# Whole TensorE tiles in place of partial ones, in a kernel of windowed attention and gated attention experts

## The chip, the cores and the metric

The kernel runs on one core of a Trainium2 chip. Its engines work side by side: TensorE (PE) multiplies matrices and writes to PSUM, VectorE (DVE), ScalarE (ACT) and GpSimd (POOL) work element by element, and SyncE (SP) issues most DMA transfers. The time is the device time of one execution in microseconds (us).

A matmul is two instructions of TensorE: the weight load (PEld) puts one operand into the array, the matmul streams the other through it. The page writes their sizes as rows*columns of the array used (32*64, 128*128), then the shape of the streamed operand (partitions x elements).

## The reference

Two stages follow each other. First a sliding window attention of 8 batches and 8 heads over 576 positions with head dimension 64; then four attention experts over the 512 joined features, of which a gate picks two for each position.

```python
# stage 1: q, k, v are (8, 8, 576, 64) in fp32
scores = (q @ k.transpose(0, 1, 3, 2)) / sqrt(64)
mask = abs(pos[:, None] - pos[None, :]) <= 32
attn = softmax(where(mask, scores, -1e9))
x = (attn @ v).transpose(0, 2, 1, 3).reshape(8, 576, 512)

# stage 2: 4 experts, head dimension 64
logits = x @ w_gate
topk, w = the two largest logits of each position, softmax of the two
for e in range(4):
    q, k, v = x @ wq[e], x @ wk[e], x @ wv[e]
    a = softmax(where(causal, -1e9, q @ k.transpose(0, 2, 1) / sqrt(64)))
    ye = a @ v @ wo[e]
    out += (e in topk) * w * ye
```

A sequence of 576 positions is four and a half tiles of 128. The half tile at the end is what most of this case is about.

## The kernel before

The work is cut into named steps, and the list `ORDER` says in which order they are issued. Each engine runs its own instructions in that order. `S.i.h` is half `h` of the window scores of head group `i` (four heads; two groups to a batch), `U` and `E` the products with v, `T` the turning of the attention's result, `QK`, `V`, `PS`, `AV`, `PT`, `Y` the expert's projections, scores, products, transposes and output, `G1` and `G3` the gate, `w18` eighteen warm-up matmuls. The digits after the colon name which of four PSUM slots (two banks each) a step gets. `load`, `turn`, `loadv` and `dup` bring q, k and v in; a load of q or k may be issued once VectorE has turned the one three head groups before.

Window scores. Keys are on the output partitions, queries stream. The four heads of a group lie on four groups of 32 partitions, and the head dimension is cut in two halves `dh`. Each entry of `BLK` is (first key, keys, first query, last query); an entry of 128 keys fills the output's 128 partitions, one of 64 keys half of them.

```python
BLK = [[[(0, 128, 0, 128)], [(128, 64, 64, 192), (192, 64, 128, 256)], [(256, 64, 192, 256)]],
       [[(256, 128, 256, 384)], [(512, 128, 448, 576)], [(384, 64, 320, 448), (448, 64, 384, 512)]]]
CUT = [0, 256, 576]

def win_scores(b, g, half):
    ...
    for blocks in BLK[half]:
        for dh in range(2):
            for k0, n, lo, hi in blocks:
                p0 = k0 % 128
                for hh in range(4):
                    r = slice(32 * hh, 32 * hh + 32)
                    nc.tensor.matmul(sl[hh // 2][p0:p0 + n, hh % 2, lo - c0:hi - c0],
                                     KT[r, dh, k0:k0 + n], QT[r, dh, lo:hi],
                                     start=(dh == 0), stop=(dh == 1), skip_group_check=True)
    for p in range(2):
        ap = A[:, 2 * p:2 * p + 2, c0:c1]
        nc.scalar.activation(ap, sl[p][:, :, 0:c1 - c0], EXP, scale=scale_att)
        # then the mask, on GpSimd (on VectorE for the first two head groups)
```

The attention's result `XN` is [128 positions, tile, 512 features]. The fifth tile has only 64 positions, so the two head groups share it: group 0 in partitions 0 to 63, group 1 in 64 to 127. Turning it, 128 features at a time:

```python
def win_turn(b, dt):                      # four times for a batch
    pt = slot("tx")...
    for t in range(4):
        nc.tensor.transpose(pt[:, 128 * t:128 * t + 128], XN[:, t, 128 * dt:128 * dt + 128], ident)
    r = slice(64 * (dt // 2), 64 * (dt // 2) + 64)
    nc.tensor.transpose(pt[:, 512:576], XN[r, 4, 128 * (dt % 2):128 * (dt % 2) + 128], ident[r, r])
    nc.scalar.copy(XTF[:, dt, 0:S], pt[:, 0:S])
    nc.gpsimd.tensor_copy(X[b][:, dt, :], XTF[:, dt, 0:S])      # bf16
```

The experts, two at a time (`j`), where the size of a tile is `nrow(t) = min(128, 576 - 128 * t)`:

```python
def moe_proj_qk(b, j, n):   # for each 288 positions: 4 matmuls, 128 weights columns, whole tiles
    ...
def moe_proj_v(b, part):    # part 0: tiles 0 to 3; part 1: tile 4, n = 64
    ...
            nc.tensor.matmul(o, XTB[:, dt, 128 * t:128 * t + n], WV[:, dt, :], ...)

def moe_scores(b, j, c):
    ...
            nc.tensor.matmul(ps[0:rows, eo, at:at + hi - lo],
                             QKE[r, 1, 128 * kt:128 * kt + nrow(kt)], QKE[r, 0, lo:hi], ...)

def moe_av(b, j):
    for eo in range(2):
        for qt in range(NQT):                       # NQT = 5
            n = nrow(qt)
            for kt in range(qt + 1):
                nk = nrow(kt)
                o = off(kt, 128 * qt)
                nc.tensor.matmul(po[0:n, eo, 65 * qt:65 * qt + 65], ATE[0:nk, eo, o:o + n],
                                 VE[0:nk, kt, 2 * j + eo, :], start=(kt == 0), stop=(kt == qt))
    # then normalised and weighted by VectorE, into OE

def moe_turn(b, j):
    for qt in range(NQT):
        n = nrow(qt)
        nc.tensor.transpose(pt[:, 128 * qt:128 * qt + n], OE[0:n, qt, :, :]..., ident_bf[:n, :n])
    nc.vector.tensor_copy(OTT[:, j, :], pt[:, 0:S])

def moe_y(b, t0):           # two tiles at a time, the fifth alone
    for t in tiles:
        n = nrow(t)
        for j in range(2):
            nc.tensor.matmul(py[0:n, t - t0, :], OTT[:, j, 128 * t:128 * t + n], WO[:, j, :], ...)
    # ScalarE copies py to ysb, SyncE sends it out
```

Of the kernel before, what the change touches and what calls it, by code (L numbers as in the profile page):

```python
# [22 lines left out]
    load.0.qn.0 load.0.kn.0 loadv.0.0 load.1.kn.0 turn.0.qn.0 load.1.qn.0 turn.0.kn.0 dup.0.0.3 dup.0.0.1  # L23
    dup.0.0.0 dup.0.0.2 load.0.qn.1 w18:2 S.0.0:01 turn.1.kn.0 load.0.kn.1 loadv.0.1 dup.0.1.1 turn.1.qn.0
    w17:2 U.0.0:1 w8:3 S.1.0:02 turn.0.qn.1 WL.q load.2.qn.0 turn.0.kn.1 dup.0.1.2 dup.0.1.0 load.2.kn.0
    w9:1 S.1.1:20 load.3.qn.0 dup.0.1.3 S.0.1:13 U.1.0:0 U.1.1:1 E.0:3 WC.q U.0.1:0 T.0.3:3 w1:1 T.0.1:0
    T.0.0:3 T.0.2:1 turn.2.qn.0 turn.2.kn.0 w8:0 QK.0.0.0:1 load.3.kn.0 WL.v S.2.0:30 turn.3.qn.0
    turn.3.kn.0 loadv.1.0 load.4.qn.0 QK.0.0.1:1 QK.0.1.0:3 S.3.0:02 PS.0.0.0:3 QK.0.1.1:1 load.4.kn.0 WC.v
    S.2.1:02 G1.0:1 PS.0.1.0:3 PS.0.0.1:0 V.0.0:2 dup.1.0.3 dup.1.0.1 G3.0 dup.1.0.0 dup.1.0.2 S.3.1:03
    V.0.1:2 turn.4.qn.0 U.2.0:1 PS.0.1.1:0 turn.4.kn.0 PS.0.0.2:3 U.2.1:2 U.3.0:0 load.5.kn.0 PS.0.1.2:3  # L30
    late.0 U.3.1:1 PS.0.0.3:2 load.5.qn.0 E.1:3 S.4.0:20 T.1.2:3 turn.5.kn.0 T.1.3:1 turn.5.qn.0 T.1.0:2
    loadv.2.0 T.1.1:0 AV.0.0:3 PS.0.1.3:0 S.4.1:21 G1.1:0 S.5.0:23 G3.1 load.6.qn.0 QK.1.0.0:1 load.8.qn.0
    dup.2.0.2 load.6.kn.0 turn.6.qn.0 V.1.0:2 load.7.kn.0 dup.2.0.0 dup.2.0.3 QK.1.0.1:0 turn.6.kn.0
    dup.2.0.1 load.8.kn.0 S.5.1:13 QK.1.1.0:2 PS.1.0.0:1 U.4.1:0 QK.1.1.1:2 PS.1.0.1:1 S.6.0:03 U.5.1:2
    PS.1.1.0:0 PT.0.0:1 E.2:3 V.1.1:2 load.7.qn.0 PS.1.0.2:0 turn.7.qn.0 U.5.0:1 S.6.1:23 U.4.0:0 loadv.3.0
    WL.o PS.1.0.3:2 load.9.kn.0 T.2.2:1 turn.7.kn.0 T.2.3:3 PS.1.1.1:2 load.10.qn.0 T.2.0:0 T.2.1:1
    turn.8.qn.0 AV.0.1:3 dup.3.0.0 S.7.0:10 dup.3.0.3 G1.2:2 PS.1.1.2:3 turn.8.kn.0 G3.2 QK.2.0.0:1
    dup.3.0.2 dup.3.0.1 V.2.0:0 S.7.1:13 QK.2.0.1:2 PS.1.1.3:1 AV.1.0:0 S.8.0:21 loadv.4.0 U.7.1:3
    load.9.qn.0 turn.9.kn.0 PS.2.0.0:0 V.2.1:2 QK.2.1.0:1 dup.4.0.0 PS.2.0.1:0 load.11.qn.0 U.6.1:3 E.3:1
    QK.2.1.1:2 PS.2.0.2:1 load.10.kn.0 WC.o U.7.0:0 U.6.0:2 PS.2.1.0:1 PT.1.0:0 T.3.3:3 load.11.kn.0 T.3.1:2  # L40
    turn.9.qn.0 T.3.0:1 dup.4.0.2 loadv.5.0 PT.0.1:3 S.8.1:20 PS.2.0.3:3 AV.1.1:1 T.3.2:0 turn.10.qn.0
    dup.4.0.3 load.12.qn.0 dup.4.0.1 turn.10.kn.0 S.9.0:32 Y.0.0:0 PT.1.1:3 PS.2.1.1:1 AV.2.0:2 PS.2.1.2:1
    QK.3.0.0:0 G1.3:3 S.9.1:01 QK.3.0.1:2 G3.3 Y.0.2:0 V.3.0:1 PS.2.1.3:0 load.12.kn.0 PS.3.0.0:3 U.9.0:2
    E.4:0 PS.3.0.1:3 QK.3.1.0:1 S.10.0:02 turn.11.kn.0 Y.0.4:1 turn.11.qn.0 QK.3.1.1:3 PS.3.0.2:2 U.9.1:0
    PS.3.1.0:3 V.3.1:1 Y.1.0:2 U.8.1:1 PS.3.0.3:3 U.8.0:0 PS.3.1.1:3 dup.5.0.2 S.10.1:12 PT.2.0:0 AV.2.1:3
    T.4.1:1 T.4.2:2 turn.12.kn.0 dup.5.0.3 loadv.6.0 T.4.0:0 turn.12.qn.0 T.4.3:1 PS.3.1.2:2 dup.6.0.1
    load.13.kn.0 Y.1.2:3 G1.4:1 S.11.0:20 V.4.0:3 G3.4 PT.2.1:0 AV.3.0:2 PS.3.1.3:3 QK.4.0.0:1 dup.5.0.1
    dup.5.0.0 S.12.0:30 QK.4.0.1:2 load.13.qn.0 Y.1.4:3 V.4.1:1 QK.4.1.0:0 PS.4.0.0:1 S.11.1:32 dup.6.0.0
    load.15.qn.0 QK.4.1.1:0 PS.4.0.1:3 PT.3.0:1 U.10.1:2 PS.4.1.0:1 U.11.0:0 PS.4.0.2:2 U.11.1:3 dup.6.0.2
    S.12.1:01 load.15.kn.0 E.5:3 U.10.0:2 PS.4.0.3:1 T.5.2:3 turn.13.kn.0 load.14.kn.0 PS.4.1.1:0 T.5.3:1  # L50
    loadv.7.0 T.5.0:2 turn.13.qn.0 Y.2.0:3 T.5.1:0 PS.4.1.2:1 AV.3.1:2 S.13.0:03 AV.4.0:1 load.14.qn.0
    PT.3.1:3 PS.4.1.3:2 QK.5.0.0:0 G1.5:2 dup.6.0.3 turn.14.kn.0 S.13.1:30 QK.5.1.0:1 QK.5.0.1:3 G3.5
    AV.4.1:1 turn.15.kn.0 PS.5.0.0:3 QK.5.1.1:2 Y.2.2:0 PS.5.0.1:1 V.5.0:3 PS.5.1.0:1 E.6:2 U.12.1:0
    PS.5.1.1:1 PS.5.0.2:2 U.13.0:3 dup.7.0.1 Y.2.4:0 turn.15.qn.0 Y.3.0:1 U.13.1:3 PS.5.1.2:0 V.5.1:2
    dup.7.0.0 U.12.0:1 PS.5.0.3:0 T.6.3:2 PT.4.0:3 T.6.2:0 T.6.0:2 turn.14.qn.0 T.6.1:3 S.15.0:01 PS.5.1.3:3
    Y.3.2:2 dup.7.0.3 G1.6:0 QK.6.0.0:3 G3.6 S.14.0:21 QK.6.1.0:3 dup.7.0.2 PT.4.1:0 S.15.1:12 QK.6.0.1:0
    U.15.0:1 S.14.1:23 PS.6.0.0:1 AV.5.0:0 V.6.0:3 PS.6.0.1:1 Y.3.4:0 QK.6.1.1:2 V.6.1:1 E.7:0 U.14.1:3
    PS.6.1.0:0 PS.6.0.2:1 U.14.0:2 U.15.1:3 PS.6.1.1:1 T.7.0:2 PT.5.0:0 T.7.3:3 T.7.1:1 PS.6.0.3:2 T.7.2:0
    AV.5.1:3 PS.6.1.2:0 Y.4.0:2 QK.7.0.0:1 PT.5.1:3 AV.6.0:2 PS.6.1.3:3 QK.7.0.1:1 Y.4.2:3 QK.7.1.0:0
    PS.7.0.0:1 Y.5.0:3 QK.7.1.1:0 PS.7.0.1:1 G1.7:2 PS.7.1.0:0 PS.7.0.2:1 AV.6.1:3 G3.7 Y.4.4:0 V.7.0:1  # L60
    PS.7.0.3:3 PS.7.1.1:0 PT.6.0:2 Y.5.2:3 V.7.1:0 PS.7.1.2:2 PT.6.1:1 AV.7.0:0 PS.7.1.3:2 Y.5.4:1 AV.7.1:0
    Y.6.0:1 PT.7.0:2 PT.7.1:2 Y.7.0:2 Y.6.2:1 Y.7.2:1 Y.6.4:2 Y.7.4:2
# [6 lines left out]
S = 576  # L69
# [6 lines left out]
def kernel(  # L76
# [30 lines left out]
    xp = ctx.enter_context(tc.tile_pool(name="xp", bufs=1))  # L107
    mp = ctx.enter_context(tc.tile_pool(name="mp", bufs=2))
    atep = ctx.enter_context(tc.tile_pool(name="atep", bufs=3))
# [91 lines left out]
    def late_constants():  # L201
        nc.scalar.copy(ident_bf, ident)

    XTF = consts.tile([128, NDT, 640], F32, name="XTF")
    nc.gpsimd.memset(XTF[:, :, S:640], 0.0)

# [37 lines left out]
    def cast_weights(n):  # L244
# [4 lines left out]
        else:  # L249
# [5 lines left out]

    BLK = [[[(0, 128, 0, 128)], [(128, 64, 64, 192), (192, 64, 128, 256)], [(256, 64, 192, 256)]],
           [[(256, 128, 256, 384)], [(512, 128, 448, 576)], [(384, 64, 320, 448), (448, 64, 384, 512)]]]
    CUT = [0, 256, 576]

    AT, X, st = {}, {}, {}  # L260
# [15 lines left out]
    def win_scores(b, g, half):  # L276
# [6 lines left out]
        for blocks in BLK[half]:  # L283
            for dh in range(2):
                for k0, n, lo, hi in blocks:
                    p0 = k0 % 128
                    for hh in range(4):
                        r = slice(32 * hh, 32 * hh + 32)
                        nc.tensor.matmul(sl[hh // 2][p0:p0 + n, hh % 2, lo - c0:hi - c0],  # L289
                                         KT[r, dh, k0:k0 + n], QT[r, dh, lo:hi],  # L290
                                         start=(dh == 0), stop=(dh == 1), skip_group_check=True)
# [42 lines left out]
    def win_turn(b, dt):  # L334
        pt = slot("tx")[:, :, :].rearrange("p a c -> p (a c)")
        for t in range(4):
            nc.tensor.transpose(pt[:, 128 * t:128 * t + 128], XN[:, t, 128 * dt:128 * dt + 128], ident)  # L337
        r = slice(64 * (dt // 2), 64 * (dt // 2) + 64)
        nc.tensor.transpose(pt[:, 512:576], XN[r, 4, 128 * (dt % 2):128 * (dt % 2) + 128], ident[r, r])  # L339
        nc.scalar.copy(XTF[:, dt, 0:S], pt[:, 0:S])  # L340
        if b not in X:
            X[b] = xp.tile([128, NDT, S], BF16, name="XTB", tag="XTB")
        nc.gpsimd.tensor_copy(X[b][:, dt, :], XTF[:, dt, 0:S])  # L343
# [53 lines left out]
    def moe_proj_qk(b, j, n):  # L397
        XTB = X[b]
        if n == 0:
            st["QK", b, j] = mp.tile([128, 2, S], BF16, name="QKE", tag="QKE")  # L400
        QKE = st["QK", b, j]
# [6 lines left out]
        o = QKE[:, n, :].rearrange("p (a c) -> p a c", c=HS)  # L408
# [5 lines left out]
    def moe_proj_v(b, part):  # L414
        XTB = X[b]
        if part == 0:
            VE = mp.tile([128, NQT, 4, 65], BF16, name="VE", tag="VE")
            nc.gpsimd.memset(VE[:, :, :, 64:65], 1.0)
            st["VE", b] = VE
        VE = st["VE", b]  # L420
        base, tiles = ((0, (0, 1, 2, 3)), (4, (4,)))[part]
        pv_ = slot("pv")
        for t in tiles:
            n = nrow(t)
            o = pv_[0:n, (t - base) // 2, 256 * (t % 2):256 * (t % 2) + 256]
            for dt in range(NDT):
                nc.tensor.matmul(o, XTB[:, dt, 128 * t:128 * t + n], WV[:, dt, :],  # L427
                                 start=(dt == 0), stop=(dt == NDT - 1))
        if part == 0:
            nc.vector.tensor_copy(VE[:, 0:4, :, 0:64],  # L430
                                  pv_[:, :, :].rearrange("p a (t e d) -> p (a t) e d", e=4, d=64))
        else:
            nc.vector.tensor_copy(VE[0:64, 4, :, 0:64],
                                  pv_[0:64, 0, 0:256].rearrange("p (e d) -> p e d", d=64))

    def moe_scores(b, j, c):
        QKE = st["QK", b, j]
        if c == 0:
            st["ATE", b, j] = atep.tile([128, 2, 1600], BF16, name="ATE", tag="ATE")
# [220 lines left out]
```

## Time and profile before

| What | Value |
|---|---|
| Time, median of three runs | 282.28 us (280.27 to 282.44) |
| Span of the profiled execution | 281.2 us |
| PE busy | 266.3 us, 95% |
| Weight loads | 192.1 us, 68% |
| DVE, ACT, POOL busy | 170.5, 162.5, 145.4 us |
| Moved by DMA | 40.59 MB, mean 144 GB/s |

The chain of work that ended last, followed back from the last instruction, is 82% TensorE. A busy time counts an instruction from its start to its end, and matmuls overlap, so that busy times of TensorE say less than the distances between starts. The page's second part cuts the span in 40 slices of 7 us and gives each engine a digit, the tenths of the slice in which it is busy; PEclk is the clock that TensorE was granted, in tenths of full speed.

### The profile page before, as it was taken

The numbers are of one execution on the slowest core, as the hardware profiler recorded it, in microseconds if no ns is written. First come the engines' busy times: TensorE is split into PE (matmuls) and PEld (weight loads), VectorE is DVE, ScalarE is ACT, GpSimd is POOL, SyncE is SP. The second block draws the span as 40 slices with busy tenths as digits, with TensorE's granted clock in tenths as the row PEclk, the third lists the DMA queues.
The fourth block names the chain that finished last, engine by engine and source line by source line (L and its number), as shares of the span: only waits on it lengthen the run. The fifth ranks groups of instructions, "written<-read, shape, count | busy, mean of one in ns | idle before, by whom it ended". The sixth has DMA issues, their size and how long they took to land.

```text
span 281.2 us, 11384 instructions
## 1 busy us (share of the span) xinstructions
PE 266.3 (95%) x4909; PEld 192.1 (68%) x4925; DVE 170.5 (61%) x538; ACT 162.5 (58%) x241; POOL 145.4 (52%) x190
## 2 busy tenths in 40 slices
PE   8979899999999999999999999999999999999762
PEld 2547677777777877777776877787677777666420
DVE  6468854875867767495847725758872364446410
ACT  0527449754657647774667278834776547486142
POOL 6110338977848783497329836774076744302100
PEclk9999999999999999999999999999999999999668
DMA  6989999999998995940549639860222000231236
GB/s 147 228 202 219 205 179 215 216 193 226 228 194 214 202 227 105 205 127 33 135 127 215 166 92 183 164 171 2 77 97 77 2 21 2 78 149 46 69 123 213
DMA packets 76562, 40.59 MB, mean 144 GB/s; under 512 B 47072, under 2 KB 71648, under 8 KB 76512
## 3 DMA queue, kind: packets, MB, share of 16 engines
q1 hardware_dynamic: 75616, 39.28, 62.3%
q8 instruction: 38, 0.62, 1.0%
q10 hardware_dynamic: 896, 0.59, 0.9%
q14 instruction: 12, 0.10, 0.1%
HBM read 30.42 MB, written 9.44 MB: 142 GB/s over the span
## 4 chain that ended last, share of the span: by engine, by line
PE 82%; DMA 8%; DVE 4%; SPq 2%; ACT 2%; issue 1%; ACTq 0%
PE sc L289 17%; PE pp L405 11%; PE po L473 9%; PE u L316 9%; PE py L506 7%; PE tx L337 7%; PE pv L427 6%; PE ps L447 5%; DMA qn<-in_q_dram 5%; PE pg L361 3%; PE pt L495 3%; PE tx L339 2%; SPq L136 2%; DMA kn<-in_k_dram 2%; PE u L327 1%
## 5 line engine op out<-in xcount | busy, mean ns | idle before, releaser
L296 POOL TENSOR_TENSOR AT<-AT,MASKP 128x512 f32<-128x512 f32 (+1 forms) x56 | 77.6, 1407 | 41.6 <-ACT AT L294 41.5
L450 ACT ACTIVATE ATE<-ps 128x1024 bf16<-128x1024 f32 (+1 forms) x64 | 52.9, 837 | 30.9 <-PE ps L447 30.6
L294 ACT ACTIVATE AT<-sc 128x512 f32<-128x512 f32 (+1 forms) x64 | 38.1, 647 | 37.5 <-PE sc L289 37.4
L289 PE MATMUL sc<-Tqn,KT 32*64 32x128 f32 (+2 forms) x2048 | 55.1, 276 | 1.7 <-DVE Tqn L273 1.0
L289 PEld LDWEIGHTS sc<-Tqn,KT 32*64 32x64 f32 (+1 forms) x2048 | 44.7, 151 | 12.1 <-issue 3.9
L316 PE MATMUL u<-VS,AT 128*64 128x65 f32 x1024 | 36.4, 224 | 0.6 <-PE u L327 0.4
L316 PEld LDWEIGHTS u<-VS,AT 128*64 128x64 f32 x1024 | 32.7, 138 | 5.5 <-issue 3.6
L454 POOL TENSOR_SCALAR_AFFINE_SELECT ATE<-ATE 128x384 bf16<-128x384 bf16 x32 | 15.9, 519 | 37.1 <-ACT ATE L450 28.2
L273 DVE STREAM_TRANSPOSE KT<-kn 128x192 f32<-128x192 f32 (+1 forms) x102 | 29.1, 385 | 3.3 <-issue 1.6
L273 DVE STREAM_TRANSPOSE Tqn<-qn 128x192 f32<-128x192 f32 (+1 forms) x102 | 29.1, 390 | 3.0 <-DMA qn<-in_q_dram 2.0
L511 ACT COPY ysb<-py 128x1024 f32<-128x1024 f32 (+1 forms) x24 | 20.7, 868 | 16.4 <-PE py L506 16.3
L343 POOL CAST XTB<-XTF 128x576 bf16<-128x576 f32 x32 | 20.8, 665 | 17.4 <-ACT wsink L214 11.3
L473 PE MATMUL po<-VE,ATE 128*128 128x65 bf16 (+2 forms) x480 | 27.5, 200 | 1.5 <-DVE OE L482 1.5
L473 PEld LDWEIGHTS <-ATE 128*128 128x128 bf16 (+2 forms) x480 | 22.0, 103 | 7.3 <-issue 2.8
L306 DVE TENSOR_TENSOR XN<-u,rs 128x512 f32<-128x512 f32 (+1 forms) x40 | 25.5, 638 | 1.4
L506 PE MATMUL py<-WO,OTT 128*128 128x512 bf16 (+1 forms) x68 | 22.3, 421 | 3.8 <-ACT ysb L511 2.2
L340 ACT COPY XTF<-tx 128x576 f32<-128x576 f32 x32 | 20.3, 642 | 9.4 <-PE tx L339 8.4
L165 POOL COPY VS<-VS 64x1024 f32<-64x1024 f32 (+1 forms) x18 | 16.9, 940 | 13.1 <-DMA VS<-in_v_dram 12.6
L447 PE MATMUL ps<-QKE 64*128 64x64 bf16 (+5 forms) x192 | 21.7, 282 | 0.6 <-DMA qn<-in_q_dram 0.5
L412 DVE CAST QKE<-pp 128x576 bf16<-128x576 f32 x16 | 12.0, 749 | 15.6 <-PE pp L405 15.2
L337 PE MATMUL tx<-ident,XN 128*128 128x128 f32 x128 | 20.9, 285 | 0.4 <-DVE rs L305 0.3
L480 DVE RECIPROCAL po<-po 128x8 f32<-128x8 f32 (+1 forms) x32 | 6.2, 193 | 24.0 <-PE po L473 17.2
(70 smaller groups left out, 330.9 us busy)
## 6 DMA issues: line engine op xcount, KB each, us to landing
kn<-in_k_dram SPq DMA_DIRECT2D x60, 144.0 KB, 4.7
qn<-in_q_dram SPq DMA_DIRECT2D x60, 144.0 KB, 5.0
out_dram<-ysb SPq DMA_DIRECT2D x16, 512.0 KB, 2.8
VS<-in_v_dram SPq DMA_DIRECT2D x21, 256.0 KB, 5.4
VS<-in_v_dram SPq DMA_DIRECT2D x14, 192.0 KB, 5.6
out_dram<-ysb SPq DMA_DIRECT2D x8, 128.0 KB, 2.2
VS<-in_v_dram SPq DMA_DIRECT2D x6, 128.0 KB, 2.7
kn<-in_k_dram SPq DMA_DIRECT2D x8, 72.0 KB, 3.4
```

Of the source, the lines that this page charges most:

```text
L273: nc.vector.transpose(T[:, dh, :].rearrange("q (a p s) -> q s a p", p=32, s=3)[:, x, a0:a1], n_[:, a0:a1, x, 32 * dh:32 * dh + 32])
L289: nc.tensor.matmul(sl[hh // 2][p0:p0 + n, hh % 2, lo - c0:hi - c0], KT[r, dh, k0:k0 + n], QT[r, dh, lo:hi], start=(dh == 0), stop=(dh == 1 ...
L294: nc.scalar.activation(ap, sl[p][:, :, 0:c1 - c0], EXP, scale=scale_att)
L296: eng.tensor_tensor(out=ap, in0=ap, in1=MASK[:, None, c0:c1].to_broadcast([128, 2, c1 - c0]), op=MULT)
L306: nc.vector.tensor_tensor(out=o, in0=u[:, :, :, 0:64], in1=rs[:, :, :, None].to_broadcast([128, n, 4, 64]), op=MULT)
L316: nc.tensor.matmul(us[64 * y:64 * y + 64, t, 65 * hh:65 * hh + 65], A[:, hh, 64 * a:64 * a + 64], V[:, a, 4 * g + hh, 0:65], start=True, s ...
L337: nc.tensor.transpose(pt[:, 128 * t:128 * t + 128], XN[:, t, 128 * dt:128 * dt + 128], ident)
L405: nc.tensor.matmul(pp[:, half, 0:HS], WQK[j][n][:, dt, :], XTB[:, dt, HS * half:HS * half + HS], start=(dt == 0), stop=(dt == NDT - 1))
L447: nc.tensor.matmul(ps[0:rows, eo, at:at + hi - lo], QKE[r, 1, 128 * kt:128 * kt + nrow(kt)], QKE[r, 0, lo:hi], start=True, stop=True)
L450: nc.scalar.activation(ATE[0:rows, :, 512 * c:512 * c + w], ps[0:rows, :, 0:w], EXP, scale=scale_moe)
L473: nc.tensor.matmul(po[0:n, eo, 65 * qt:65 * qt + 65], ATE[0:nk, eo, o:o + n], VE[0:nk, kt, 2 * j + eo, :], start=(kt == 0), stop=(kt == qt))
L506: nc.tensor.matmul(py[0:n, t - t0, :], OTT[:, j, 128 * t:128 * t + n], WO[:, j, :], start=(j == 0), stop=(j == 1))
```

## The change

Three things are done, all to let TensorE keep one tiling over longer stretches.

The expert steps use whole tiles of 128 throughout. Their buffers are padded to 640 positions, allocated once, and the pads set to zero at the start, so that the fifth tile runs like the other four; what the pad yields is not read.

The window scores are cut into blocks of 64 keys only, and these come in pairs of equal query ranges, one for the lower and one for the upper 64 output partitions.

The turning of the attention's result is done by whole transposes: sixteen for the first four tiles, eight for each head group, and two for the fifth tile, in which both groups are turned together. A step `TE` is added for the latter, and a group's turning no longer waits for the fifth tile.

The order of the steps is new, to fit.

```diff
+    XTB = consts.tile([128, NDT, 640], BF16, name="XTB")
+    QKS = [consts.tile([128, 2, 640], BF16, name=f"QKE{n}") for n in range(2)]
+    VES = [consts.tile([128, NQT, 4, 65], BF16, name=f"VE{n}") for n in range(2)]
+    ATS = [consts.tile([128, 2, 1664], BF16, name=f"ATE{n}") for n in range(3)]
+    OES = [consts.tile([128, NQT, 2, 64], BF16, name=f"OE{n}") for n in range(2)]
+    OTS = [consts.tile([128, 2, 640], BF16, name=f"OTT{n}") for n in range(2)]
+    def zero_pads():
+        nc.gpsimd.memset(XTB[:, :, S:640], 0.0)
+        ...                                   # ATS, QKS, OES, OTS; ones in VES
-    BLK = [[[(0, 128, 0, 128)], [(128, 64, 64, 192), (192, 64, 128, 256)], [(256, 64, 192, 256)]],
-           [[(256, 128, 256, 384)], [(512, 128, 448, 576)], [(384, 64, 320, 448), (448, 64, 384, 512)]]]
+    BLK = [[[(128, 64, 192), (64, 0, 128)], [(0, 0, 64), (192, 128, 192)], [(256, 192, 256), (192, 192, 256)]],
+           [[(384, 320, 448), (320, 256, 384)], [(512, 448, 576), (448, 384, 512)],
+            [(256, 256, 320), (576, 512, 576)]]]
...
-                        nc.tensor.matmul(sl[hh // 2][p0:p0 + n, hh % 2, lo - c0:hi - c0],
-                                         KT[r, dh, k0:k0 + n], QT[r, dh, lo:hi],
+                        nc.tensor.matmul(sl[hh // 2][p0:p0 + 64, hh % 2, lo - c0:hi - c0],
+                                         KT[r, dh, k0:k0 + 64], QT[r, dh, lo:hi],
...
-    def win_turn(b, dt):                      # as shown above
+    def win_turn(b, g):
+        pt = slot("tx")
+        for y in range(2):
+            for t in range(4):
+                nc.tensor.transpose(pt[:, y, 128 * t:128 * t + 128],
+                                    XN[:, t, 256 * g + 128 * y:256 * g + 128 * y + 128], ident)
+        for y in range(2):
+            nc.scalar.copy(XTF[:, 2 * g + y, 0:512], pt[:, y, :])
+            nc.gpsimd.tensor_copy(XTB[:, 2 * g + y, 0:512], XTF[:, 2 * g + y, 0:512])
+    def win_turn_end(b):
+        pt = slot("te")[:, 0, 0:256]
+        for y in range(2):
+            nc.tensor.transpose(pt[:, 128 * y:128 * y + 128], XN[:, 4, 128 * y:128 * y + 128], ident)
+        nc.scalar.copy(XTF[:, :, 512:576].rearrange("p (g y) c -> p y g c", y=2),
+                       pt.rearrange("p (y g c) -> p y g c", y=2, g=2))
+        nc.gpsimd.tensor_copy(XTB[:, :, 512:576], XTF[:, :, 512:576])
...
-                nc.tensor.matmul(o, XTB[:, dt, 128 * t:128 * t + n], WV[:, dt, :],
+                nc.tensor.matmul(o, XTB[:, dt, 128 * t:128 * t + 128], WV[:, dt, :],
...
-                                 QKE[r, 1, 128 * kt:128 * kt + nrow(kt)], QKE[r, 0, lo:hi],
+                                 QKE[r, 1, 128 * kt:128 * kt + 128], QKE[r, 0, lo:hi],
...
-                    nc.tensor.matmul(po[0:n, eo, 65 * qt:65 * qt + 65], ATE[0:nk, eo, o:o + n],
-                                     VE[0:nk, kt, 2 * j + eo, :], start=(kt == 0), stop=(kt == qt))
+                    nc.tensor.matmul(po[:, eo, 65 * qt:65 * qt + 65], ATE[:, eo, o:o + 128],
+                                     VE[:, kt, 2 * j + eo, :], start=(kt == 0), stop=(kt == qt))
...
-            nc.tensor.transpose(pt[:, 128 * qt:128 * qt + n], OE[0:n, qt, :, :].rearrange("p e d -> p (e d)"),
-                                ident_bf[:n, :n])
+            nc.tensor.transpose(pt[:, 128 * qt:128 * qt + 128], OE[:, qt, :, :].rearrange("p e d -> p (e d)"),
+                                ident_bf)
...
-                nc.tensor.matmul(py[0:n, t - t0, :], OTT[:, j, 128 * t:128 * t + n], WO[:, j, :],
+                nc.tensor.matmul(py[:, t - t0, :], OTT[:, j, 128 * t:128 * t + 128], WO[:, j, :],
```

The list `ORDER` is replaced as a whole. Its start, in both kernels:

```diff
-    load.0.qn.0 load.0.kn.0 loadv.0.0 load.1.kn.0 turn.0.qn.0 load.1.qn.0 turn.0.kn.0 dup.0.0.3 dup.0.0.1
-    dup.0.0.0 dup.0.0.2 load.0.qn.1 w18:2 S.0.0:01 turn.1.kn.0 load.0.kn.1 loadv.0.1 dup.0.1.1 turn.1.qn.0
-    w17:2 U.0.0:1 w8:3 S.1.0:02 turn.0.qn.1 WL.q load.2.qn.0 turn.0.kn.1 dup.0.1.2 dup.0.1.0 load.2.kn.0
-    w9:1 S.1.1:20 load.3.qn.0 dup.0.1.3 S.0.1:13 U.1.0:0 U.1.1:1 E.0:3 WC.q U.0.1:0 T.0.3:3 w1:1 T.0.1:0
-    T.0.0:3 T.0.2:1 turn.2.qn.0 turn.2.kn.0 w8:0 QK.0.0.0:1 load.3.kn.0 WL.v S.2.0:30 turn.3.qn.0
+    load.0.kn.0 load.0.qn.0 load.1.qn.0 turn.0.kn.0 loadv.0.0 turn.0.qn.0 load.0.qn.1 late.0 load.1.kn.0
+    dup.0.0.0 turn.1.qn.0 dup.0.0.3 load.0.kn.1 w18:2 S.0.0:01 loadv.0.1 turn.0.qn.1 turn.1.kn.0 turn.0.kn.1
+    w38:2 S.1.0:10 S.0.1:23 load.2.kn.0 dup.0.0.2 turn.2.kn.0 load.3.qn.0 WL.v load.2.qn.0 w4:1 S.1.1:20
+    dup.0.1.3 dup.0.0.1 dup.0.1.2 dup.0.1.0 U.0.1:3 U.0.0:2 dup.0.1.1 WL.q U.1.0:0 U.1.1:3 E.0:2 WC.v
+    turn.2.qn.0 T.0.0:0 turn.3.qn.0 T.0.1:3 TE.0:2 w8:1 S.2.0:23 load.3.kn.0 V.0.0:0 G1.0:3 WC.q turn.3.kn.0
+    S.2.1:02 QK.0.0.0:1 S.3.0:20 QK.0.0.1:1 loadv.1.0 load.4.kn.0 QK.0.1.0:2 load.4.qn.0 G3.0 dup.1.0.3
...
```

## The prediction

> **What bounds the kernel now.** I read the page's busy shares first, then its forty slices, then a table of busy time by 35 us stages, then the order of TensorE's work inside one batch, and last the waits.
>
> ```profile
> PE 266.3 (95%) x4909; PEld 192.1 (68%) x4925; DVE 170.5 (61%) x538; ACT 162.5 (58%) x241; POOL 145.4 (52%) x190
> PE   8979899999999999999999999999999999999762
> PEclk9999999999999999999999999999999999999668
> DMA  6989999999998995940549639860222000231236
> ```
>
> TensorE (PE) is busy from the second slice to the last few at the full clock; no other engine passes 61%. But DMA is full as well for the first 120 us. The stage table says the same (us of the stretch, busy time and number of instructions of PE, weight loads, VectorE, ScalarE, GpSimd, then clock, DMA share, GB/s):
>
> ```profile
> 35.00:70.00 35.00, 34.15 (x801) 26.98 (x800) 22.30 (x78) 22.29 (x37) 25.35 (x28) 1.00 1.09 205
> 70.00:105.00 35.00, 34.81 (x772) 27.12 (x769) 25.06 (x78) 21.11 (x31) 26.04 (x31) 1.00 1.04 213
> 210.00:245.00 35.00, 34.68 (x663) 26.25 (x664) 14.73 (x44) 20.37 (x31) 20.01 (x26) 1.00 0.10 36
> ```
>
> So from 35 us (first projection) to about 259 us the end is set by the sum of TensorE's blocks, one after another: 224 us. A matmul's record is about 200 to 370 ns long whatever it costs, because records overlap; the cost of a block is the distance from its start to the next block's start. The order of instructions in time on TensorE (start, length, line, shape, count):
>
> ```profile
> 150.30 0.27 PE L339 MATMUL tx<-ident,XN 64*128 64x64 f32 x1
> 150.50 0.66 PE L337 MATMUL tx<-ident,XN 128*128 128x128 f32 x4
> 151.09 0.27 PE L339 MATMUL tx<-ident,XN 64*128 64x64 f32 x1
> 151.29 0.66 PE L337 MATMUL tx<-ident,XN 128*128 128x128 f32 x4
> ...
> 157.77 0.52 PE L495 MATMUL pt<-ident_bf,OE 128*128 128x128 bf16 x5
> 158.22 1.66 PE L473 MATMUL po<-VE,ATE 128*128 128x65 bf16 x30
> 159.68 0.24 PE L447 MATMUL ps<-QKE 64*64 64x64 bf16 x2
> 159.86 1.16 PE L405 MATMUL pp<-XTB,WQ 128*128 128x288 bf16 x8
> 160.95 1.59 PE L289 MATMUL sc<-Tqn,KT 32*128 32x128 f32 x64
> ```
>
> Four whole transposes take 0.59 us (150.50 to 151.09), and the single quarter-size one 0.20 more (151.09 to 151.29). Record by record, in the expert product at 158.22 (30 matmuls, 1.46 us) most starts are 29 to 31 ns apart, but each step into or out of a matmul with only 64 rows or 64 output columns is 122 to 147 ns: five such steps within the block and one after the two small matmuls that follow it. In the window scores at 160.95 (64 records, 1.52 us to the next block) there is one step of 200 ns where the 32x128 tile gives way to the 32x64 one. These steps are what the change goes after.
>
> [...] the trace has 29 to 31 and, for the bf16 transposes at 157.77, 56. [...] the fp32 record here is 273 ns, but successive ones start 109 ns apart, and that is what counts. [...] In this trace eight 32x64 score matmuls start 6.6 ns apart and the next eight follow 110 ns after the first. [...]
>
> **The change part by part**, TensorE time per block, switch at its end included.
>
> Window scores, half 0 (1.52 us, as above) has a lone 32x128 block, one pair of 32x64 blocks of 128 queries, and a lone 32x64 block of 64 queries. Half 1 (1.73 us in most places of the chain of work) has two lone 32x128 blocks and one pair. After, all are pairs: half 0 has one of 128 and two of 64 queries, half 1 two of 128 and one of 64. A block or pair is four groups (two halves of the head dimension, two passes for fp32); a group takes 110 ns at 128 queries, and at 64 queries 58 ns, read from the lone block. Half 0: a first step of 160 and three of 110 make 0.49, then 4 x 58 = 0.23 twice, and about 0.15 for the switch at the end: 1.10. Half 1: 0.49 + 0.44 + 0.23 + 0.15 = 1.31. Saved 0.42 + 0.42, sixteen times: 13.4 us. The records rise from 2048 to 3072.
>
> Expert products: five steps fewer at some 95 ns above the usual 30, and two starts of 52 ns become 30: 1.46 - 0.52 = 0.94, which is 30 x 30 ns and a slower start. With a switch of 0.1 behind it where the next block has another tiling, half the time, 0.98 instead of the usual 1.60: 0.62 x 16 = 9.9 us.
>
> Attention turned: 4 x (0.59 + 0.20) = 3.16 us a batch becomes 18 whole transposes, 18 x 0.109 = 1.96, plus about 0.07 at each of three beginnings: 2.2. Saved 0.96 x 8 = 7.7 us. ScalarE and GpSimd copies keep their volume (two of 512 columns for each half and one of 4 x 64, instead of four of 576), so I count nothing there.
>
> Expert transposes: 0.46 becomes 5 x 56 ns and a little, 0.30: 0.16 x 16 = 2.6 us. The small value projection: 0.55 to 0.45, and the last output tile 0.55 to 0.45: 0.2 x 8 = 1.6 us. The last expert score block keeps its two matmuls: nothing.
>
> The sum is 35.2 us. Not on the path: the scores of the first two head groups, which stand in the first 35 us among warm-up matmuls while the loads arrive (2 x 0.84 = 1.7). That leaves 33.5 us, and 282.3 - 33.5 = 248.8 if TensorE stays as dense as now.
>
> The added memsets (a dozen small ones on GpSimd, once) lie in the same first 35 us, and the per-batch memset of the ones column goes. The new order of steps has a few more warm-up matmuls (68 instead of 61), among loads that are awaited anyway.
>
> **What comes back.** First, DMA. The wait that already shows is this one:
>
> ```profile
> 55.80 0.22 PE L447 MATMUL ps<-QKE 64*64 64x64 bf16 x2 [0.46 <-DMA qn<-in_q_dram]
> ```
>
> The fifth head group's loads landed at 52.2 us and its scores start at 56.6, after VectorE's turning. To then some 10 MB are needed (five q/k loads of 1.18 MB, two of v, the weights), and at 205 GB/s that takes 49 us plus issue and turning: it cannot come much sooner. The new order has about 17 us of TensorE work between its first projection (I expect it at 33 us) and that block, so some 4 us of waiting appear near 50 us. Later, a batch needs 3 x 1.18 MB of input, 17 us at that rate, against some 25 us of TensorE, so loads catch up by the eighth group or so. Second, the other engines: VectorE's 25.1 us of the 35 in the second stage become 25.1 in about 30, and four PSUM slots turn over faster. I estimate 1 to 2 us for such waits over the whole span. 248.8 + 4 + 1 = 253.8, or 254.
>
> **The rivals.** (a) The narrow pairs don't run eight abreast at 58 ns. In the lone 64-query block, matmuls start some 14 to 17 ns apart, and no stretch of this trace sustains a load and a matmul in less than 13.7 ns. If that is a limit and not the stream, a 64-query group of eight takes about 116 ns; three such pairs per head group cost 3 x 4 x 58 = 0.7 us more, 11 us in all: 265. For it: that regular stagger. Against it: within a burst the starts are 6.6 ns apart, weight loads included. I give it one in five. (b) DMA or the in-order engines become the bound: then the total would stick near 265 to 270. For it: the full DMA of the first 120 us. Against it: 40.6 MB at 205 GB/s are 198 us, and in the last 105 us its share is low. One in ten. (c) The clock falls back because TensorE now waits more (the last three slices show a clock of 6 to 8 tenths beside idle time). It would make any stall of (b) dearer[...]; one in twenty, 260 to 275. (d) The new order hides more of the start and end than I count: 245.
>
> **Range and chances.** 254 us, from 246 (start and tail shorten too, no DMA wait) to 264 (rival a nearly in full). Every term removes TensorE time from a span in which TensorE is the bound; to lose the 2% line, five sixths of 33.5 us would have to come back. Faster by over 2%: 0.96; within: 0.03; slower: 0.01.
>
> **What would show it.** Right: one expert product block 0.94 to 1.04 us from start to next start, with no 120 ns steps; T blocks of eight transposes near 0.9 us; score halves near 1.1 and 1.3; PE still above 90% busy, with DMA the longest wait near 50 us. Wrong: score halves at 1.5 (rival a), PE idle spread over the middle with DMA, ScalarE or GpSimd named as releaser (rival b), PEclk below 9 ahead of the tail (rival c). The prediction also fails if zero-padded whole tiles start at more than 30 ns.

## The result, and the profile after

| | Before | After |
|---|---|---|
| Median | 281.81 us (280.27 to 282.44) | 269.94 us (267.16 to 274.08) |
| Ratio to before | 1 | 0.955 (95% interval 0.946 to 0.965) |
| Span of the profiled execution | 281.2 us | 269.0 us |
| Instructions of the program | 11384 | 13457 |

Medians are over all executions of a kernel; the ratios leave disturbed ones out.

The change makes the kernel faster, by 12 us and not by the 28 us forecast; the time lies above the stated range. The busy shares, the slices and the instruction queue of the page after:

```profile
PE 242.7 (90%) x5940; PEld 187.0 (70%) x5940; DVE 171.0 (64%) x538; ACT 160.2 (60%) x247; POOL 147.8 (55%) x202
PE   7796899898789979969999899999999999999752
PEclk9999599999889999998999999999999999999998
DMA  6999999999997659930799524937955000222227
q8 instruction: 46, 0.75, 1.3%
```

TensorE's row of nines has got holes, all in the first 23 slices; later it is as full as before. The clock even dips to 5 tenths once, beside such a hole. The busy time of every other engine changed by less than 2.5 us. The stage table says where (us of the stretch, busy us and instructions of PE, weight loads, VectorE, ScalarE, GpSimd, then clock, DMA share, GB/s):

```profile
70.00:105.00 35.00, 31.16 (x967) 26.30 (x967) 24.52 (x78) 20.50 (x31) 26.07 (x30) 0.95 0.82 176
...
210.00:245.00 35.00, 35.00 (x765) 27.47 (x764) 22.23 (x72) 23.32 (x38) 19.33 (x28) 1.00 0.12 40
```

Between 70 and 105 us PE lost 3.8 us of 35; before, it lost 0.2. The table of waits names the releaser (engine and line, what for, us in total, times, longest):

```profile
PEld sc L305 <- issue: 10.7, 18, 2.4
...
PE sc L305 <- issue: 6.3, 5, 2.2
```

"issue" means that TensorE waited for no semaphore, no other engine and no load that the profile shows. In the kernel before, the score lines had at most 0.6 us of it at a time:

```profile
PEld sc L289 <- issue: 3.9, 15, 0.6
```

The order in time on TensorE shows two of the holes, which end at 71.88 and at 77.36 (the bracket is the idle time ahead of the line):

```profile
67.00 1.55 PE L305 MATMUL sc<-Tqn,KT 32*64 32x128 f32 x96
68.48 1.09 PE L482 MATMUL po<-VE,ATE 128*128 128x65 bf16 x30
69.50 0.20 PE L458 MATMUL ps<-QKE 64*128 64x64 bf16 x2
69.63 0.47 PE L384 MATMUL pg<-XTF,WG 128*32 128x160 f32 x4
71.88 2.27 PE L384 MATMUL pg<-XTF,WG 128*32 128x160 f32 x28 [1.79 <-issue]
74.08 1.98 PE L305 MATMUL sc<-Tqn,KT 32*64 32x128 f32 x96
75.99 0.66 PE L425 MATMUL pp<-XTB,WQ 128*128 128x288 bf16 x4
77.36 0.67 PE L425 MATMUL pp<-XTB,WQ 128*128 128x288 bf16 x4 [0.70 <-issue]
```

Both fall in the middle of a step, among matmuls that have nothing to wait for. That is the clue. Counting every instruction of TensorE from the start of the program, its sequencer's included, thirteen distances of over 0.4 us between neighbours have no wait to explain them and lie outside the warm-up; the second of the pair follows instruction 705, 961, 1473, 1729, 2497, 3009, 3265, 4545, 5057, 5313, 5569, 7105 or 8385. Each is 193 more than a multiple of 256. The instruction queue moved 46 packets of 16384 bytes for 11880 records of PE and PEld, about one for every 256, which makes 64 bytes for an instruction. From this I take it that TensorE stood still because its next instructions were not there yet. What is said of this fetch here and below is read off the packets and the instruction counts of these traces.

Seen against the packets: in all thirteen cases the packet starts 1.4 to 3.6 us after TensorE steps into a new block of 256, takes 1.0 to 1.5 us, and TensorE goes on 1.39 to 1.65 us after the packet's end. As I read it, in these cases only one block was fetched ahead, and only once the block before it was begun. At 67.03 us a block began, its instructions were used up after 2.77 us, and the next could start only after 4.85. The thirteen distances add up to 16.6 us; before, there were two such, 1.1 us together (0.65 and 0.41).

The three longest of these waits, of 2.38, 2.09 and 2.46 us, end at 26.05, 71.88 and 119.37 us, and soon after each of them the granted clock was at half (the last three numbers are clock, DMA share and GB/s):

```profile
27.60:34.40 6.80, 5.69 (x104) 5.60 (x106) 3.28 (x7) 3.42 (x5) 0.00 (x0) 0.50 1.02 183
72.00:75.40 3.40, 3.40 (x86) 2.89 (x89) 1.00 (x5) 0.00 (x0) 1.24 (x2) 0.50 0.97 211
119.80:123.20 3.40, 3.40 (x24) 1.81 (x30) 1.04 (x2) 1.36 (x3) 2.56 (x2) 0.50 0.02 5
```

None of the other ten waits, of up to 1.62 us, was followed by such a drop (one of them lies in the first stretch). What ran at half clock took longer: the scores at 74.08, for one, at a mean clock of 0.65, lasted 1.91 us to the next block instead of 1.37.

The second finding is in the score blocks, where nothing disturbs them (half 0 at 216.39, half 1 at 222.00):

```profile
216.39 1.44 PE L305 MATMUL sc<-Tqn,KT 32*64 32x128 f32 x96
217.76 0.60 PE L509 MATMUL py<-WO,OTT 128*128 128x512 bf16 x2
...
222.00 1.55 PE L305 MATMUL sc<-Tqn,KT 32*64 32x128 f32 x96
223.47 0.34 PE L384 MATMUL pg<-XTF,WG 128*32 128x160 f32 x4
```

They last 1.37 and 1.47 us, where 1.10 and 1.31 were forecast. Record by record, the first 37 of half 0 come as forecast, eight at a time, 110 ns from one eight to the next; after that, matmuls come one or two at a time, mostly 16 to 17 ns or about half of that apart (the 16.7 and 8.3 ns of the expectations below are these steps, and their 2.1 us are 256 of the shorter). The mean of these later steps is 12.1 ns in half 0 and 13.8 in half 1.

### The profile page after: what moved, and what is told of

The parts are those of the page before. It is cut to its first block, busy times and chain, and to the rows that moved or that the text cites. A ratio compares the mean times of both kernels' runs of the same rounds, so it can differ in the third digit from the quotient of the medians.

```text
span 269.0 us, 13457 instructions
## 1 busy us (share of the span) xinstructions
PE 242.7 (90%) x5940; PEld 187.0 (70%) x5940; DVE 171.0 (64%) x538; ACT 160.2 (60%) x247; POOL 147.8 (55%) x202
## 5 line engine op out<-in xcount | busy, mean ns | idle before, releaser
L305 PE MATMUL sc<-Tqn,KT 32*64 32x128 f32 (+1 forms) x3072 | 49.6, 258 | 6.3 <-issue 6.3
L305 PEld LDWEIGHTS sc<-Tqn,KT 32*64 32x64 f32 x3072 | 44.5, 132 | 14.3 <-issue 10.7
L358 POOL CAST XTB<-XTF 128x512 bf16<-128x512 f32 x32 | 18.6, 612 | 17.0 <-ACT XTF L357 16.9
L161 POOL COPY VS<-VS 64x1024 f32<-64x1024 f32 (+1 forms) x18 | 17.4, 968 | 11.8 <-DMA VS<-in_v_dram 11.2
L509 PE MATMUL py<-WO,OTT 128*128 128x512 bf16 x80 | 20.8, 380 | 2.9 <-ACT ysb L514 2.4
L357 ACT COPY XTF<-tx 128x512 f32<-128x512 f32 x32 | 17.0, 595 | 8.9 <-PE tx L354 8.5
L229 PE MATMUL warm<-WARM 128*128 128x512 bf16 x68 | 18.2, 430 | 3.3 <-ACT wsink L230 1.9
L441 PE MATMUL pv<-WV,XTB 128*128 128x256 bf16 x160 | 20.5, 276 | 0.2 <-DVE OE L491 0.2
L432 DVE CAST QKE<-pp 128x576 bf16<-128x576 f32 x16 | 12.1, 755 | 12.8 <-PE pp L425 12.8
L425 PE MATMUL pp<-XTB,WQ 128*128 128x288 bf16 x128 | 18.7, 287 | 1.5 <-issue 1.5
L458 PE MATMUL ps<-QKE 64*128 64x64 bf16 (+4 forms) x192 | 19.9, 282 | 0.1
L425 PE MATMUL pp<-XTB,WK 128*128 128x288 bf16 x128 | 19.4, 297 | 0.0
```

The costliest lines, as they stand in the source:

```text
L305: nc.tensor.matmul(sl[hh // 2][p0:p0 + 64, hh % 2, lo - c0:hi - c0], KT[r, dh, k0:k0 + 64], QT[r, dh, lo:hi], start=(dh == 0), stop=(dh == ...
L425: nc.tensor.matmul(pp[:, half, 0:HS], WQK[j][n][:, dt, :], XTB[:, dt, HS * half:HS * half + HS], start=(dt == 0), stop=(dt == NDT - 1))
L441: nc.tensor.matmul(o, XTB[:, dt, 128 * t:128 * t + 128], WV[:, dt, :], start=(dt == 0), stop=(dt == NDT - 1))
L458: nc.tensor.matmul(ps[:, eo, at:at + hi - lo], QKE[r, 1, 128 * kt:128 * kt + 128], QKE[r, 0, lo:hi], start=True, stop=True)
L509: nc.tensor.matmul(py[:, t - t0, :], OTT[:, j, 128 * t:128 * t + 128], WO[:, j, :], start=(j == 0), stop=(j == 1))
```

## The experiments

The theory, from here on "instruction supply": the pairs raise the score blocks from 64 to 96 matmul records with as many weight loads, 2048 instructions more in all. By this theory TensorE pays for them twice, by the rate at which they are issued within the block, and by fetches that no longer hide behind 256 instructions. The rivals: the new order of steps or late data make the holes; and the pairs are bound by the stream and not by the issue.

**Old score blocks in the changed kernel.**

```diff
-    BLK = [[[(128, 64, 192), (64, 0, 128)], [(0, 0, 64), (192, 128, 192)], ...
+    BLK = [[[(0, 128, 0, 128)], [(128, 64, 64, 192), (192, 64, 128, 256)], [(256, 64, 192, 256)]], ...
-                for k0, lo, hi in blocks:
+                for k0, n, lo, hi in blocks:
```

> The changed kernel with the window score blocks of before (64 matmul records a half instead of 96), all else and the order of steps as changed. Theory 'instruction supply' (the 2048 added instructions of the scores make TensorE wait for its own instructions, which are fetched 256 at a time by DMA behind the data loads, and are issued at about 8.3 ns each): the idle times of TensorE that end with 'issue' fall from 17 us to under 4 us, the score halves go back to 1.52 and 1.73 us (6 us lost), and the time is 258 to 263 us, below the changed kernel's 270. Rival 'new order / late data' (the idle times come from the order of steps and from loads that arrive late): the idle times stay, and the slower score halves add up, 274 to 277 us.

Measured: 259.87 us, ratio to before 0.921 (0.912 to 0.930). The time and the slower score halves are those that the theory forecast. TensorE's slices in the page:

```profile
PE   7599999999999999999999999999999999999652
```

The same place in the order in time as above:

```profile
62.36 1.79 PE L304 MATMUL sc<-Tqn,KT 32*128 32x128 f32 x64
64.09 1.09 PE L481 MATMUL po<-VE,ATE 128*128 128x65 bf16 x30
65.11 0.20 PE L457 MATMUL ps<-QKE 64*128 64x64 bf16 x2
65.24 1.29 PE L383 MATMUL pg<-XTF,WG 128*32 128x160 f32 x32
66.47 1.83 PE L304 MATMUL sc<-Tqn,KT 32*128 32x128 f32 x64
```

The holes are gone but for two short ones at steps between blocks of 256, 0.70 us at 94 us and 0.67 at 195 us, and the gate's 32 matmuls run through in 1.2 us. The scores are slower than the pairs, 1.73 us for a half 1 against 1.48, and the kernel is 10 us faster all the same. Order and loads are those of the changed kernel, so they did not make the holes. This version beats both kernels; it is the one to keep.

**The pairs alone, in the kernel before.** The edit is the reverse, made in the kernel before.

> The kernel before with only the new score blocks (96 records a half), its own order of steps and partial tiles kept. Theory 'instruction supply': score halves near 1.4 and 1.5 us give back 6 us, but TensorE now waits for instructions at several places in the first 150 us, 5 to 12 us in all, so the time is 279 to 288 us. Rival 'new order / late data': nothing of that sort appears under the old order, and the time falls by the full 6 us or more, to 275 us or less.

Measured: 285.52 us, ratio 1.014 (1.006 to 1.022), slower than before by 0.6 to 2.2%. Score halves last 1.38 and 1.48 us where undisturbed, so 6 us came off the blocks, and more than that came back. Two of its waits:

```profile
PEld sc L290 <- issue: 6.5, 18, 2.1
...
PE u L317 <- issue: 4.1, 3, 1.8
```

Six of its seven distances without a wait to explain them, spaced by multiples of 256 but for a few records that the trace lacks, add up to 9.5 us. So the holes come with the pairs, under the old order too.

**No q and k loads after the third head group.** The later groups turn the first three groups' data again, so their scores are those of the first three.

```diff
+        if i > 2:
+            nat[nm, b, g] = nat[nm, (i - 3) // 2, (i - 3) % 2]
+            return
```

> The changed kernel without the loads of q and k after the third head group (the later groups turn the first three groups' data again; all instructions of TensorE stay). DMA is then far from full. Theory 'instruction supply', fetch delayed by data traffic: the idle times of TensorE that end with 'issue' fall from 17 us to under 4 us, while the score halves stay at 1.37 and 1.48 us; the time is 250 to 258 us. If the fetch were too slow by itself, whatever else DMA moves, the idle times would stay above 10 us and the time near 266 us.

Measured: 263.78 us, in one execution. This forecast failed, and it was the theory's own. TensorE's and DMA's slices:

```profile
PE   7599599999999979979999999999999999999652
DMA  6989999004700071002065128349320000223236
```

From the eighth slice to the twentieth DMA is mostly idle, yet the unexplained distances still come to about 11 us against the changed kernel's 16.6, two of them near 112 and 117 us, where the DMA row shows 0. In the stretch that the missing loads emptied, from 46 to 131 us, they are 6.2 us against 10.4. So with the loads gone the waits in that stretch are 4.2 us shorter, and 6.2 us of them stay: data traffic lengthens them, and is not what makes them. I had put the waits down to a full DMA because they stood where DMA was full; but that is where most of the score blocks stand as well.

**The fetch by itself.** A kernel of nothing but score pairs on constants: twenty halves in quiet, then twenty beside the loads of all q and k.

```diff
+        for n in range(20):
+            scores(n % 2, P[0:2])          # quiet
+        ...                                # 32 loads of q and k, released here
+        for n in range(20):
+            scores(n % 2, P[2:4])          # beside the loads
```

> Nothing but score blocks of the new kind (20 halves of 96 matmuls, 3840 instructions, twice), on constants, with no other engine in their way; the first twenty while DMA moves nothing but instructions, the second twenty beside loads of all of q and k. Nothing of the reference is computed. Theory 'fetch by itself': also in quiet the next 256 instructions come only some 3.5 to 5 us after the fetch before was done with, more than the 2.1 us that they take to issue, so the first twenty halves last 52 to 75 us and the second twenty about 60 to 85. Rival 'data traffic delays the fetch': the first twenty run at the issue rate, 32 to 36 us, and only the second twenty are slower, 60 us or more.

Measured: the first twenty halves end near 56 us after starting at 3.5, the second near 124. Two stretches of the order in time, quiet and beside the loads:

```profile
12.02 1.77 PE L49 MATMUL sc<-QT,KT 32*64 32x128 f32 x128 [1.54 <-issue]
15.47 1.99 PE L49 MATMUL sc<-QT,KT 32*64 32x64 f32 x128 [1.68 <-issue]
18.93 1.87 PE L49 MATMUL sc<-QT,KT 32*64 32x128 f32 x128 [1.46 <-issue]
...
80.77 2.67 PE L49 MATMUL sc<-QT,KT 32*64 32x128 f32 x128 [1.23 <-issue]
85.60 3.41 PE L49 MATMUL sc<-QT,KT 32*64 32x64 f32 x128 [2.15 <-issue]
90.70 3.04 PE L49 MATMUL sc<-QT,KT 32*64 32x128 f32 x128 [1.69 <-issue]
```

Each line is 128 matmuls and their 128 weight loads, one block of 256, then a wait. In quiet (DMA share 0.02 from 12 to 48 us) the blocks start 3.45 to 4.0 us apart (15.47 - 12.02 = 3.45); beside the loads (1.03 from 60 to 120 us) 4.0 to 5.1 apart, once 6.5. In quiet a block needs only 1.8 to 2.0 us to run at the full clock, so the fetch sets the pace, by itself: 256 instructions in 3.45 us are 13.5 ns for one, in 4.5 us 17.6. The rival "data traffic" expected 32 to 36 us for the first twenty.

The clock is not the cause of the longer distance. Its mean was 0.98 from 12 to 48 us and 0.66 from 60 to 120; it was at half in parts of both passes, and there a block ran for up to 3.4 us; but the quiet block that began at 48.48 at half clock was followed by the next after 3.45 us all the same, and three blocks beside the loads that ran through at the full clock in 1.77, 1.77 and 1.87 us, from 67.94, 95.25 and 119.10, by theirs after only 4.28, 6.47 and 4.55. The packets show where the time goes. In quiet, one starts 0.9 to 1.2 us after TensorE steps into a block, takes 0.9 to 1.4, and TensorE goes on 1.3 to 1.5 us after its end. Beside the loads the last two are nearly the same, 1.0 to 1.4 and 1.3 to 1.7, and the start comes after 1.3 to 3.6 us. So beside the loads it is the start of the fetch that comes later.

**The second pass cut short.** The queries of the second half of the head dimension are halved in number; that part of the scores is left out.

```diff
+                    hi = lo + (hi - lo) // (1 + dh)
```

> The changed kernel with the queries of the second half of the head dimension cut to half their number (that part of the scores is left out); as many instructions, a quarter less streamed in the score blocks. Theory 'issue bound': score halves within 0.05 us of 1.37 and 1.48, because 96 weight loads and 96 matmuls are supplied at about 16.7 ns a pair. Rival 'stream bound': they fall by 0.16 to 0.27 us each.

Measured: 267.89 us, with undisturbed score halves of 1.26 and 1.37 us, 0.11 less each. Neither forecast is met: a quarter less stream saves less than the stream alone would, and more than nothing. The records show a limit of each kind in turn. With the shorter stream the 33rd matmul starts 383 ns after the first instead of 487, so up to there TensorE follows the stream. But the next weight loads, the 34th in the changed kernel and the 35th here, start 458 to 460 ns after the first matmul in every undisturbed half of both: so from there on it is not the stream that sets the time, and I put it down to the supply. What sets the later mean, 12.1 and 13.8 ns in the changed kernel and 10.4 and 12.2 here, is not shown; a fixed 16.7 ns for a load and a matmul it is not.

**Pairs where there is room.** Old blocks for the first ten head groups, pairs for the last six.

```diff
-        for blocks in BLK[half]:
+        for blocks in (PAIRS if 2 * b + g >= 10 else BLK)[half]:
```

> The changed kernel with the score blocks of before for the first ten head groups and the new pairs for the last six, where the changed kernel's trace has few waits for instructions. Theory: the six groups give 6 x 0.40 = 2.4 us against old blocks everywhere (259.9 us) and lose about 1 us to waits: 257 to 260 us. If waits move to wherever the pairs are, 260 us or more.

Measured: 259.70 us (254.98 to 261.62), ratio 0.927 (0.921 to 0.934). The traced execution has one unexplained distance of over 0.4 us, at 92 us, and the late halves last 1.37 and 1.48. The waits don't follow the pairs there, but a gain of some 2 us against old blocks everywhere is not shown: its five executions spread over 6.6 us, the two ratios' intervals overlap, and the two were measured on different chips.

**Pairs in the second half of each group only.**

```diff
-        for blocks in BLK[half]:
+        for blocks in (PAIRS if half == 1 else BLK)[half]:
```

> The changed kernel with the old blocks in the first half of each head group's scores and the new pairs in the second half, 0.25 us shorter each. It saves 16 x 0.25 = 4 us of scores against old blocks everywhere and adds 1024 instructions, four fetches; theory 'instruction supply' gives back 2 to 6 us in waits that end with 'issue': 258 to 263 us. If only back-to-back pairs overrun the fetch, the gain stays: 256 to 257 us.

Measured: 264.05 us (260.10 to 266.59), ratio 0.930 (0.920 to 0.940), against 259.87 with old blocks everywhere. Seven distances without a wait, each again 193 more than a multiple of 256, add up to 7.4 us, more than the 4 us saved in the blocks. The forecast allowed 2 to 6 us for them; the waits were underrated by a little.

**Partial tiles in the expert products.** Old score blocks, and `moe_av` as before.

```diff
-                    nc.tensor.matmul(po[:, eo, 65 * qt:65 * qt + 65], ATE[:, eo, o:o + 128],
-                                     VE[:, kt, 2 * j + eo, :], ...
+                    nc.tensor.matmul(po[0:n, eo, 65 * qt:65 * qt + 65], ATE[0:nk, eo, o:o + n],
+                                     VE[0:nk, kt, 2 * j + eo, :], ...
```

> The changed kernel with the old score blocks everywhere and, besides, the expert products with partial tiles as before (64 rows or 64 output columns for the last tile). If a step between tilings costs what I took it for, 16 x 0.62 = 9.9 us come back on top of 259.9: 267 to 272 us. If the wider products were hidden behind some other bound by then, 260 to 264 us.

Measured: 272.24 us, ratio 0.968 (0.962 to 0.975), against 259.87 with whole tiles. The blocks go from a mean of 0.97 back to 1.60 us, 16 x 0.63 = 10.1 us. The other 2.3 us of the difference between the medians are more than the blocks account for; one wait for instructions of 1.7 us in this trace, where the run with whole tiles has 0.7 at the same instruction, is part of it, and the clock was at half from 254.6 us to the end of this trace. The padding of the products works as intended, and it is worth 10.1 of the 22 us by which the version with old score blocks is faster than the kernel before.

## Why the prediction was wrong

Term by term, by its own sum:

| Term | Forecast | Measured, block by block |
|---|---|---|
| Window scores | 13.4 us saved | 16 x (1.52 - 1.37 + 1.73 - 1.48) = 6.4 |
| Expert products | 9.9 | 16 x (1.60 - 0.97) = 10.1, with the usual 1.60 (the mean before was 1.56) |
| Attention turned | 7.7 | two blocks of about 0.93 and one of 0.26: 8 x (3.16 - 2.12) = 8.3 |
| Expert transposes | 2.6 | 16 x (0.46 - 0.28) = 2.9 |
| Small value and output tiles | 1.6 | about 1.7 |
| Sum | 35.2 | 29.4 |
| Waits for instructions | none | 16.6 - 1.1 = 15.5 lost |
| Half clock after the long waits | none | about 3.3 lost, an estimate |
| Waits for loads and other engines | 5 lost | not seen where they were expected |

The estimate of 3.3 us compares the blocks in the two later stretches at half clock, 72.0 to 75.4 and 119.8 to 123.2 us, with their like at the full clock; the first stretch lies among the first loads and is left out. 29.4 - 0.8 (scores of the first two head groups, 2 x 0.40) - 15.5 - 3.3 = 9.8 us, and 12 were measured. About 2 us stay unaccounted for. The tail may hold part of them: in the trace before, the clock was at half from 262.5 to 272.7 us, in the trace after only from 266.6 on.

**The step that failed first** is the one that reads "282.3 - 33.5 = 248.8 if TensorE stays as dense as now". It did not: thirteen waits for instructions took 16.6 us. The prediction counted the new instructions ("The records rise from 2048 to 3072") and gave them no price; and it looked for new waits among loads, PSUM slots and engines only. The page before had what was needed, an instruction queue with 38 packets for 9834 records of PE and PEld:

```profile
q8 instruction: 38, 0.62, 1.0%
```

In its records there are two distances of 0.65 and 0.41 us with no releaser, 512 instructions apart to within the few records that are missing. These waits of 1.1 us together were the sign of the limit that later took 16.6.

**The second** is a size: "at 64 queries 58 ns, read from the lone block". The lone block has four matmuls in 58 ns, and the pair needs eight. The prediction saw this as rival (a), with the stagger of 14 to 17 ns as the sign and a price of 11 us, and gave it one in five. It was two thirds right: 0.27 + 0.17 = 0.44 us more per head group than forecast, 7 us in all, because in the halves at 216.39 and 222.00 the first 37 matmuls still started 6.6 ns apart within each eight, and only those after them at a mean of 12.1 and 13.8. "Within a burst the starts are 6.6 ns apart" was the wrong evidence against it. It was read from bursts of eight, and the same 6.6 ns did not last in a half of 96.

**Rival (b)**, DMA or the in-order engines as the bound, came true in its number (265 to 270 us) and not in its cause. The 4 us of waiting for loads near 50 us did not show up as such: the changed kernel's trace has no load as a releaser of TensorE there. Its start is slower instead: the attention's result is turned from 35.8 us on instead of 29.9, and 3.8 us of that are two waits for instructions. **Rival (c)** came true in part, behind another cause: the clock fell to half after the three waits of over 2 us, for 6.8, 3.4 and 3.4 us, and what ran there took longer, by an estimated 3.3 us on the path. With the old score blocks, where no such waits stand, the clock row shows no dip between its third slice and its last.

**Right** was the price of a change of tiling. The four terms that rest on it were forecast within 12%; the 1.6 us one I checked on single blocks only. Taken without the pairs, and without the 5 us that it allowed for other waits, the prediction's sum is good: 248.8 plus the 28 x 0.42 = 11.8 us that the old score blocks keep on the path makes 260.6, and that kernel took 259.9.

**Open.** Why a fetch takes 3.45 us in quiet, of which the packet itself takes 0.9 to 1.4, is not known, and whether TensorE could be made to fetch more than one block ahead was not tried. How much of the late pairs' gain is real is not settled.

## What to carry to other kernels

Count the instructions of the bound engine beside its busy time. In the changed kernel TensorE used up five blocks of 256 in less than 3.0 us, and stood still for 1.05 to 2.46 us after each of them; of five used up in 3.1 to 3.4 us one was followed by such a wait, and even a block that lasted 5.6 us was, its packet having started only 3.6 us into it. An fp32 matmul counts four instructions, two loads and two passes (the scores' 1536 matmuls in the changed program are 3072 records, with 3072 loads). Here a cut that shortened the stream by adding small matmuls lost (the pairs alone, ratio 1.014), and padding that removed changes of tiling at the same count won (259.87 us with whole tiles in the products, 272.24 with partial ones). Idle time that ended with "issue", in the middle of a step and at the same count modulo 256, I put down to the fetch.

## What the runs showed that I had not expected

- With nothing but score pairs, blocks of 256 instructions started 3.45 to 4.0 us apart in quiet and mostly 4.0 to 5.1 us with DMA full; in the changed kernel, leaving out most loads of q and k took away only about a third of the waits (16.6 us to 11).
- Eight 32x64 tiles side by side started 6.6 ns apart within the first 37 matmuls of the halves at 216.39 and 222.00; after those the mean distance was 12.1 ns in the first and 13.8 in the second.
- After each of the three waits of over 2 us the clock was at half for 3.4 or 6.8 us; none of the ten shorter ones was followed by such a drop.
- A change of tiling cost much the same in fp32 and bf16, in transposes and products. In the products it was a step of 122 to 147 ns against 29 to 31, and with five or six of them gone a block of 30 matmuls was 0.63 us shorter. In the expert transposes two steps of 132 and 152 ns against 56 went, 0.18 us; in the attention's 1.04 us a batch went with eight changes, 0.13 each, the small transposes' own time included.
